# Four inner products of the first matrix product in two levels, with units that accumulate on banks filled by ScalarE and VectorE

## The chip, the cores and the metric

The kernel runs on one core of one Trainium2 chip. The metric is the device time of one execution in microseconds (us). Its engines are TensorE (PE, matrix products; PEld is its loading of weights), VectorE (DVE), ScalarE (ACT), GpSimd (POOL) and SyncE (SP). The last two issue most of the DMAs here.

## What is computed

```python
# q, k, v: (B, H, S, D) = (4, 8, 768, 64), lam: (8,), all fp32
for b in range(S // 64):                           # lightning attention, block by block
    intra = (qb @ kb^T * Dmask) @ vb               # Dmask[i, j] = lam^(i - j) for i >= j
    inter = (qb * lam^(pos + 1)) @ kv_state
    out[block] = intra + inter
    kv_state = lam^64 * kv_state + (kb * lam^(63 - pos))^T @ vb
x = out as (B*S, H*D) = (3072, 512)
h = x @ w_in                                       # w_in  (512, 2048): the first matrix product
g = h - tanh(h)
return g @ w_out                                   # w_out (2048, 512): the second matrix product
```

## The kernel before

**Groups and units.** The kernel takes the sequence in 128-token blocks. Six groups (`NG`) of 512 tokens, one block of each of the four batches, go one after another: `g` is 0 to 5. The hidden width of 2048 is cut into four units (`NU`, `u` is 0 to 3) of 512. Group 0 is the startup, with plain products while the weights arrive. Group 1 uses one-level products throughout. Groups 2 to 5 (`g >= GI`) are the steady state.

**Seven products for eight.** Both matrix products are computed by the scheme with seven block products P1 to P7 in place of eight. The operands of each are sums and differences of quarters: `FACT` names them, S1 to S4 on one side and T1 to T4 on the other. The four result quarters are called 11, 12, 21 and 22. With P1 as a base, C11 = P1 + P2, and P1 + P6 is shared: C12 adds P5 and P3 to it, C22 adds P7 and P5, C21 adds P7 and P4. `hidden(g, c)` is the buffer in SBUF of quarter c of the hidden layer; a one-level product is done there unit by unit, in `up(g, u, n)`, with 8 matmul records of 256 columns a unit.

**Two levels.** A block product can be split by the same scheme once more. It is then seven steps of 8 records of 128 columns, in the order `STEPS` = 1, 2, 6, 5, 7, 3, 4, over all four units at once. For the second matrix product, `down_twice` (L697) does so for P3 to P7 (`TWICE`), and `down` (L684) keeps P1 and P2 at one level. For the first, `inner_steps(g, n, tag)` (L518) does so for P2 and P4 (`INNER`, groups from 2 on). Its result goes into `hidden` quarter 11 or 21 through ScalarE copies and VectorE additions. `inner_weights` (in group 1) makes the factors of the weights, four VectorE operations of 128x128 a unit and product, and stores them in `fine_in`; `inner_tokens` makes those of the tokens, four operations a product.

**The steady state.** At the seam of two groups, P3 of the second product of group g alternates with the inner steps of P2 of group g+1 (`in_turn`); then come the inner steps of P4, with P1, P6 and P5 of unit 0 between them. The unit loop follows, in the order P7, P3 for a unit and P6, P5, P1 for the next. P5 of a unit goes to the PSUM bank `z`, P3 is accumulated upon it, and P1, P6 and P7 are accumulated on `ya` or `yb` by the parity of u. VectorE adds the pieces up in `hidden`, ScalarE takes the tanh (L454) and VectorE subtracts it (L455). After P3 the sums S1 and S2 of the second product are made (L482 and the line behind it). Then follows the second product, P1 (`every(down(g, 1))` as the last act of the unit loop, in bank `ya`), P2 in bank `w`, P4, P5, P6 and P7. Between them run the pieces of attention for group g+1, by halves of two batches each: `att_transpose` (for g >= 2 a VectorE transpose of blocks that 16 DMAs on SyncE's queue load per tile, L143), `att_scores` (L333), `att_out`, `att_state` and the token sums `att_sums`. Transposes and scores of batches 0 and 1 stand in the unit loop (`run(p0[u - 2:u - 1])`).

**PSUM.** There are eight banks of 128x512: `ya`, `yb`, `z` and `w` with one buffer each, and four under the tag `att`, which attention and the inner steps take in turn.

**Weights.** The factors for the second product lie in DRAM (`factors` for one level, `fine` and `fine_in` for two levels). `piece` (L620, L623) issues their loads of 256 KB on GpSimd's queue, in the order of `stream`, into a ring `wb` of seven tiles (`RING`), as the tile used seven pieces earlier comes free. The two-level factors themselves are made in groups 1 and 2 by `load_quarters` and `factors_twice`: VectorE subtracts quarters of `factors`, and GpSimd stores each result in `fine` (L604, L614). In group 2 these quarters go through the same ring, and the stream has all twelve of them ahead of P1's four pieces.

**What orders the work.** The program's text gives the order by generators that are advanced step by step. A scheduler may move an instruction of an engine past another when their operands allow, save where `keep_in_program_order` ties it. So P7 and P3 of a unit, for instance, stand around the matmuls of other units in the built order.

Of the kernel before, what the change touches and what calls it, by code (L numbers as in the profile page):

```python
# [24 lines left out]
def kernel(  # L25
# [32 lines left out]
    nc = tc.nc  # L58
# [127 lines left out]
    TWICE = (3, 5, 6, 4, 7)  # L186
    fine = dram.tile([len(TWICE), len(SUB), 128, NU, 128], F32, name="fine")

    fine_in = dram.tile([2, 3, 128, NU, 128], F32, name="fine_in")
    w_in_u = moe_w_in.rearrange("k (a n) -> k a n", a=2)  # L190
    blocks = [("in", u, i) for u in range(NU) for i in range(KI)] + [("out", kt, a) for kt in range(KH)
                                                                    for a in range(2)]
# [244 lines left out]
    def up(g, u, n):  # L437
        a, bname = FACT[n]
        wt = {"A11": w1[u][:, 0:2, 0], "A12": w1[u][:, 2:4, 0], "S3": w1[u][:, 0:2, 1], "A22": w1[u][:, 2:4, 1],
              "S1": ws[u][:, 0], "S2": ws[u][:, 1], "S4": ws[u][:, 2]}[a]  # L440
        x = xt[g][bname] if bname != "B11" else xt[g, 0][:, 0:2]
        key = ("up", g, u)
        t, first = product_bank(key, n)
        for m in range(2):
            for kt in range(2):
                nc.tensor.matmul(out=t[:, m, :], lhsT=wt[:, kt, ts(m, 128)], rhs=x[:, kt, :],  # L446
                                 start=first and m == 0 and kt == 0, stop=kt == 1, skip_group_check=True)

        def dst(c):
            return hidden(g, c)[:, u]  # L450

        def finish(c, src):
            th = work.tile([128, 2, HB], F32, name="th", tag="th")
            nc.scalar.activation(th, src, AF.Tanh)  # L454
            nc.vector.tensor_tensor(dst(c), src, th, op=AL.subtract)  # L455

        y, z, w = (banks[key, x].rearrange("q (m c) -> q m c", m=2) if (key, x) in banks else None for x in "yzw")
        if g >= GI and n == 1:
            nc.vector.tensor_tensor(dst(11), dst(11), y, op=AL.add)  # L459
            finish(11, dst(11))  # L460
        elif g >= GI and n == 5:
            nc.scalar.activation(dst(22), z, AF.Copy)  # L462
        elif g >= GI and n == 7:
            nc.vector.tensor_tensor(dst(22), dst(22), y, op=AL.add)
            nc.vector.tensor_tensor(dst(21), dst(21), y, op=AL.add)
            finish(22, dst(22))
            finish(21, dst(21))
        elif n == 1:
            nc.scalar.activation(dst(11), y, AF.Copy)
        elif n == 2:  # L470
            nc.vector.tensor_tensor(dst(11), dst(11), w, op=AL.add)
            finish(11, dst(11))
        elif n == 6:
            nc.scalar.activation(dst(12), y, AF.Copy)
        elif n == 7:
            nc.scalar.activation(dst(22), y, AF.Copy)
            nc.vector.tensor_tensor(dst(22), dst(22), z, op=AL.add)
            finish(22, dst(22))
        elif n == 4:
            finish(21, y)  # L480
        elif n == 3:
            nc.vector.tensor_tensor(dst(12), dst(12), z, op=AL.add)  # L482
            finish(12, dst(12))

            nc.vector.tensor_tensor(dst("S1"), dst(12), dst(22), op=AL.add)
            nc.vector.tensor_tensor(dst(12), dst(11), dst(12), op=AL.subtract)

    INNER = (2, 4)  # L490
    toks = {}

    def a_quarter(n, u, i, k):
        return w1[u][:, 2 + k, INNER.index(n), ts(i, 128)]

    def inner_weights(u):
        for n in INNER:
# [8 lines left out]
    def inner_tokens(g):  # L506
        for n in INNER:
            x = xt[g][FACT[n][1]]
# [9 lines left out]
    def inner_steps(g, n, tag):  # L518

        y, w, z, r5 = bank("y3", tag, 1), bank("w3", "att", 4), bank("z3", "att", 4), otile("r5")  # L520
        out4 = hidden(g, 11 if n == 2 else 21)
        c11, c12, c21, c22 = (out4[:, :, i, ts(j, 128)] for i in range(2) for j in range(2))
        for x in STEPS:
            b = toks[g, n][x]
            wb = piece(g, ("in", n), x) if x in (3, 5, 6) else None
            dst = w if x == 2 else z if x in (3, 5) else y
            for u in range(NU):
                a = wb.rearrange("p m c -> p (m c)")[:, ts(u, 128)] if wb is not None else a_quarter(
                    n, u, *{1: (0, 0), 2: (0, 1), 7: (1, 0), 4: (1, 1)}[x])
                nc.tensor.matmul(out=dst[:, ts(u, 128)], lhsT=a, rhs=b, start=x in (1, 2, 5) and u == 0, stop=True,  # L530
                                 skip_group_check=True)
# [20 lines left out]
    def in_turn(g):  # L552

        if twice(g, 3):
            return [a for x in STEPS for a in (("down", x), ("in", x))]
        return [("down", 0), ("in", 1), ("in", 2), ("down", 1), ("in", 6), ("in", 5), ("down", 2), ("in", 7), ("in", 3),
                ("down", 3), ("in", 4)]

    def pieces_of(g):
        if g >= GI:  # L560
            yield from ((g, ("in", 4), x) for x in (6, 5, 3))
        if g == 2:
            yield from ((g, ("quarter", t), x) for t in (2, 3, 4) for x in range(4))
        for n in (1, 2, 4, 5, 6, 7):
            yield from ((g, n, x) for x in (SUB if twice(g, n) else range(NU)))
        if g == NG - 1:
            yield from ((g, 3, x) for x in range(NU))
# [1 line left out]
        for kind, x in in_turn(g):  # L569
            if kind == "down":  # L570
                yield g, 3, x
            elif x in (3, 5, 6):
                yield g + 1, ("in", 2), x

    stream = [x for g in range(1, NG) for x in pieces_of(g)]
    sent = {"n": 0}
# [66 lines left out]

    def down(g, n):

        if n in (1, 2):
            t, first = product_bank(("down", g), n)
        else:
            t, first = bank("plain", "w" if n == 7 else "z", 1).rearrange("q (m c) -> q m c", m=2), True
# [240 lines left out]
    late["pool"] = ctx.enter_context(tc.tile_pool(name="late", bufs=1))  # L890


    turns = {1: (0, ((0, 7), (1, 14))), 2: (7 * NU, ((2, 1), (3, 5), (4, 9)))}
    made, making = [], {}
    load_quarters(0)
    load_quarters(1)
    up(1, 0, 1)
    for g in range(1, NG):
        last = g == NG - 1
        p0, p1 = attention(g + 1) if not last else ([], [])  # L900
        for u in range(NU):
            for n in (2, 6, 5, 7, 1, 4, 3) if g < GI else (1, 7, 3) if u == 0 else (6, 5, 1, 7, 3) if u + 1 < NU else (
                    6, 5, 7, 1, 3):
                if n != 1:
                    up(g, u, n)
                elif u + 1 < NU:
                    up(g, u + 1, 1)
                else:
                    every(down(g, 1))
                if g == 1 and u < 2 and n == 5:  # L910
                    sums_in(u + 2)
                if g in turns:
                    made.append(n)
                    step = len(made) - turns[g][0]
                    for t, first in turns[g][1]:
                        if step == first:
                            if t > 1:
                                load_quarters(t)
                            making[t] = factors_twice(t)
                        if first <= step < first + 4:  # L920
                            next(making[t])
            if g == GI - 1:
                inner_weights(u)
            if not last and u > 1:
                run(p0[u - 2:u - 1])
        if twice(g, 4):
            sums_twice(g, 4)
        every(down(g, 2))
# [23 lines left out]
        every(p2)  # L952
        every(p3)
        p4 = inner_steps(g + 1, 4, "yb")
        for n in (None, None, 1, None, None, 6, None, None, 5, None):
# [35 lines left out]
```

## Time and profile before

| | |
|---|---|
| time, median of 3 runs | 672.54 us (670.41 to 673.64) |
| span of the profiled execution | 668.3 us |
| that execution's span and the median run | 4.2 us apart |
| PE busy | 655.9 us (98%), 4920 records |
| DVE busy | 466.4 us (70%), 839 instructions |
| ACT busy | 212.4 us (32%), 402 instructions |
| POOL busy | 210.3 us (31%), 365 instructions |
| mean granted TensorE clock | 1.000 |
| bytes moved | 128.82 MB, 193 GB/s over the span |

Two records of PE stand for one fp32 matmul of the program; "busy" counts the time in which an instruction of that engine was in execution. The span runs from the first to the last instruction, and the time of a run includes what lies around the span. Group 0 takes the first 108 us or so, and a steady group about 119 us.

### The profile page before, as it was taken

The numbers are of one execution on the slowest core, as the hardware profiler recorded it, in microseconds if no ns is written. First come the engines' busy times: TensorE is split into PE (matmuls) and PEld (weight loads), VectorE is DVE, ScalarE is ACT, GpSimd is POOL, SyncE is SP. The second block draws the span as 40 slices with busy tenths as digits, with TensorE's granted clock in tenths as the row PEclk, the third lists the DMA queues.
The fourth block names the chain that finished last, engine by engine and source line by source line (L and its number), as shares of the span: only waits on it lengthen the run. The fifth ranks groups of instructions, "written<-read, shape, count | busy, mean of one in ns | idle before, by whom it ended". The sixth has DMA issues, their size and how long they took to land.

```text
span 668.3 us, 13066 instructions
## 1 busy us (share of the span) xinstructions
PE 655.9 (98%) x4920; PEld 594.3 (89%) x4920; DVE 466.4 (70%) x839; ACT 212.4 (32%) x402; POOL 210.3 (31%) x365
## 2 busy tenths in 40 slices
PE   8899899999999999999999999999999999999998
PEld 7688788888888989888999988999988899988897
DVE  4477886746988762599885379987368877357753
ACT  4796835503321111341112343112233112234110
POOL 0001444734522433244435101344300245400351
PEclk9999999999999999999999999999999999999999
DMA  9989887968755977568899543698830576610494
GB/s 211 221 218 259 251 320 227 331 172 239 222 136 144 234 184 209 137 210 260 231 269 279 143 75 81 163 275 252 221 67 18 157 237 220 220 35 0 124 298 162
DMA packets 163038, 128.82 MB, mean 193 GB/s; under 512 B 134176, under 2 KB 135328, under 8 KB 162976
## 3 DMA queue, kind: packets, MB, share of 16 engines
q0 software_dynamic: 29296, 96.49, 44.5%
q1 hardware_dynamic: 133536, 31.50, 24.2%
q8 instruction: 39, 0.64, 0.4%
q14 instruction: 23, 0.19, 0.1%
q10 hardware_dynamic: 144, 0.00, 0.0%
HBM read 103.55 MB, written 24.38 MB: 191 GB/s over the span
## 4 chain that ended last, share of the span: by engine, by line
PE 75%; issue 11%; DMA 5%; POOL 4%; ACT 2%; SPq 2%; DVE 1%; POOLq 0%; DVEq 0%; ACTq 0%
PE y L446 13%; PE z L446 8%; PE y L708 8%; PE acc L792 7%; PE zw L708 6%; PE h L763 5%; PE w L655 4%; PE y L655 4%; PE y L530 4%; PE plain L655 3%; PE sp L340 3%; POOL wb L620 3%; PE op L394 2%; DMA raw<-in_moe_w_in_dram 2%; PE z L530 2%
## 5 line engine op out<-in xcount | busy, mean ns | idle before, releaser
L620 POOL DMA_DIRECT2D wb<-fine x147 | 79.1, 539 | 113.8 <-PE y L708 49.6
L623 POOL DMA_DIRECT2D wb<-factors x56 | 30.3, 541 | 156.0 <-PE y L655 99.7
L454 ACT ACTIVATE th<-g 128x512 f32<-128x512 f32 x76 | 47.6, 630 | 99.1 <-DVE g L459 33.2
L446 PE MATMUL y<-xt,w 128*128 128x256 f32 x320 | 74.0, 380 | 0.0
L446 PEld LDWEIGHTS y<-xt,w 128*128 128x128 f32 x320 | 59.9, 190 | 8.5 <-ACT g L534 0.9
L711 ACT ACTIVATE q<-y 128x128 f32<-128x128 f32 x84 | 23.3, 277 | 129.9 <-PE y L708 126.2
L455 DVE TENSOR_TENSOR g<-g,th 128x512 f32<-128x512 f32 x76 | 51.8, 687 | 16.8 <-ACT th L454 16.7
L763 PE MATMUL h<-xt,w 128*128 128x256 f32 x256 | 57.9, 382 | 3.0 <-DVE w L284 3.0
L763 PEld LDWEIGHTS h<-xt,w 128*128 128x128 f32 x256 | 47.7, 190 | 10.7 <-DVE w L284 3.4
L708 PE MATMUL y<-wb,g 128*128 128x128 f32 x384 | 51.1, 278 | 0.0
L708 PEld LDWEIGHTS y<-wb,g 128*128 128x128 f32 x384 | 46.4, 192 | 1.2 <-issue 0.3
L446 PE MATMUL z<-tt,ws 128*128 128x256 f32 x160 | 38.0, 380 | 0.0
L446 PE MATMUL z<-xt,ws 128*128 128x256 f32 x160 | 37.9, 380 | 0.0
L446 PE MATMUL y<-tt,ws 128*128 128x256 f32 x160 | 37.8, 379 | 0.0
L655 PE MATMUL y<-wb,g 128*128 128x256 f32 x160 | 35.6, 379 | 0.5 <-PE y L446 0.5
L655 PE MATMUL w<-wb,g 128*128 128x256 f32 x160 | 35.8, 382 | 0.0
L205 POOL DMA_DIRECT2D raw<-in_moe_w_out_dram x16 | 8.7, 547 | 85.0 <-ACT r L281 60.6
L344 DVE TENSOR_TENSOR ss<-sp,mask 128x512 f32<-128x512 f32 x48 | 30.9, 681 | 6.3 <-PE sp L340 6.3
L655 PEld LDWEIGHTS y<-wb,g 128*128 128x128 f32 x160 | 30.3, 190 | 5.0 <-PE y L446 0.9
L446 PEld LDWEIGHTS z<-xt,ws 128*128 128x128 f32 x160 | 30.3, 190 | 4.3 <-ACT g L462 0.2
L655 PEld LDWEIGHTS w<-wb,g 128*128 128x128 f32 x160 | 30.1, 190 | 4.4
L708 PE MATMUL zw<-wb,g 128*128 128x128 f32 x256 | 33.8, 275 | 0.0
(198 smaller groups left out, 1348.7 us busy)
## 6 DMA issues: line engine op xcount, KB each, us to landing
wb<-fine POOLq DMA_DIRECT2D x147, 256.0 KB, 4.0
wb<-factors POOLq DMA_DIRECT2D x68, 256.0 KB, 4.1
raw<-in_moe_w_out_dram POOLq DMA_DIRECT2D x16, 512.0 KB, 5.8
v_nat<-in_v_dram SPq DMA_DIRECT2D x24, 256.0 KB, 5.1
fine<-wt POOLq DMA_DIRECT2D x24, 256.0 KB, 4.8
wb<-fine_in POOLq DMA_DIRECT2D x24, 256.0 KB, 4.1
k_nat<-in_k_dram SPq DMA_DIRECT2D x20, 256.0 KB, 4.9
raw<-in_moe_w_in_dram SPq DMA_DIRECT2D x8, 512.0 KB, 5.7
```

The lines of the kernel that those rows point to most:

```text
L344: tied(g == 0, nc.vector.tensor_tensor(ss[:, j], sp[j], mask[:, j], op=AL.mult))
L446: nc.tensor.matmul(out=t[:, m, :], lhsT=wt[:, kt, ts(m, 128)], rhs=x[:, kt, :], start=first and m == 0 and kt == 0, stop=kt == 1, skip_gro ...
L454: nc.scalar.activation(th, src, AF.Tanh)
L455: nc.vector.tensor_tensor(dst(c), src, th, op=AL.subtract)
L530: nc.tensor.matmul(out=dst[:, ts(u, 128)], lhsT=a, rhs=b, start=x in (1, 2, 5) and u == 0, stop=True, skip_group_check=True)
L620: nc.gpsimd.dma_start(out=t.rearrange("p m c -> p (m c)"), in_=fine[TWICE.index(n_), SUB.index(x_)].rearrange("p u c -> p (u c)"))
L623: nc.gpsimd.dma_start(out=t, in_=factors[XAT[FACT[n_][1]]][:, 2 * x_:2 * x_ + 2, :])
L655: nc.tensor.matmul(out=t[:, m, :], lhsT=a[:, u, kt, ts(m, 128)], rhs=wb[:, kt, :], start=first and u == 0 and m == 0 and kt == 0, stop=u = ...
L708: nc.tensor.matmul(out=dst, lhsT=a[:, u, :], rhs=wb[:, ts(u, 128)], start=x in (1, 2) and u == 0, stop=u == NU - 1, skip_group_check=True)
L711: nc.scalar.activation(keep, dst, AF.Copy)
L763: tied(u == 0, nc.tensor.matmul(out=hm[c][:, m, :], lhsT=w1[u][:, i, a, ts(m, 128)], rhs=xt[0, t][:, i, :], start=m == 0 and i == 0, stop= ...
L792: nc.tensor.matmul(out=acc[n][:, r, :], lhsT=a[:, ts(r, 128)], rhs=b, start=kt == 0 and r == 0, stop=kt == KH - 1, skip_group_check=True)
```

## The change

P1 and P5 of the first product join P2 and P4 in two levels for the groups 2 to 5: `INNER` becomes (1, 5, 2, 4). In the unit loop of these groups only P6, P3 and P7 are left, in a new function `seeded`.

- For P6 of a unit, ScalarE copies quarter 12 of `hidden`, where the inner steps of P1 landed, into bank `ya` or `yb`, and the matmuls accumulate on that. VectorE then writes the bank's content plus quarter 22 (where P5 landed) into a second bank, `z` for even and `w` for odd units, and P3's matmuls accumulate there. P7 accumulates on the first bank. The second bank's content goes through tanh, and a VectorE subtraction that reads the bank writes C12.
- C11 is P1's landing (12) plus P2's landing (11). It is finished by VectorE and ScalarE (`n == 11`) beside the inner steps of P4.
- P1 of the second product takes an `att` bank, and its four units are spread over the unit loop. The pieces of `stream` in group 2 follow that order: P1's piece, four quarters, P1's next piece.
- The inner steps of P1 alternate with P3 of the second product, those of P5 and P2 alternate with each other, and P6 of units 0 and 1 and P3 of unit 0 stand among the steps of P4.
- The transposes and scores of batches 0 and 1 move from the unit loop of group g to the seam ahead of it, as `early_pieces` for group g+2.

In the built program, PE has 128 matmuls of 256 columns fewer and 224 of 128 columns more (2492 to 2588 in all), VectorE has 88 additions, subtractions and the like more (733 to 821), ScalarE 16 instructions more (401 to 417), GpSimd 32 DMAs more (359 to 391), and SyncE as many as before.

```diff
-    fine_in = dram.tile([2, 3, 128, NU, 128], F32, name="fine_in")
+    INNER = (1, 5, 2, 4)
+    fine_in = dram.tile([len(INNER), 3, 128, NU, 128], F32, name="fine_in")
...
-    INNER = (2, 4)
+    LAND = {1: 12, 5: 22, 2: 11, 4: 21}
+    BANKS = {1: ("yb", "w", "att"), 5: ("ya", "att", "z"), 2: ("yb", "w", "att"), 4: ("att", "att", "att")}
+    def seeded(g, u, n):
...
+        if n == 11:
+            nc.vector.tensor_tensor(dst(11), dst(11), dst(12), op=AL.add)
+            finish(11, dst(11))
+            return
+        if n == 6:
+            banks[g, u, "y"] = bank("y", "yb" if u % 2 else "ya", 1).rearrange("q (m c) -> q m c", m=2)
+            nc.scalar.activation(banks[g, u, "y"], dst(12), AF.Copy)
+        y = banks[g, u, "y"]
+        t = banks[g, u, "z"] if n == 3 else y
...
+        for m in range(2):
+            for kt in range(2):
+                nc.tensor.matmul(out=t[:, m, :], lhsT=wt[:, kt, ts(m, 128)], rhs=x[:, kt, :], start=False,
+                                 stop=kt == 1, skip_group_check=True)
+        if n == 6:
+            z = banks[g, u, "z"] = bank("zs", "w" if u % 2 else "z", 1).rearrange("q (m c) -> q m c", m=2)
+            nc.vector.tensor_tensor(z, y, dst(22), op=AL.add)
+        elif n == 3:
+            finish(12, t)
+        else:
+            nc.vector.tensor_tensor(dst(22), dst(22), y, op=AL.add)
+            nc.vector.tensor_tensor(dst(21), dst(21), y, op=AL.add)
+            finish(22, dst(22))
+            finish(21, dst(21))
+    def seeded_sums(g, u):
+        g11, g12, g22, s1 = (hidden(g, c)[:, u] for c in (11, 12, 22, "S1"))
+        nc.vector.tensor_tensor(s1, g12, g22, op=AL.add)
+        nc.vector.tensor_tensor(g12, g11, g12, op=AL.subtract)
...
     def pieces_of(g):
         if g >= GI:
             yield from ((g, ("in", 4), x) for x in (6, 5, 3))
-        if g == 2:
-            yield from ((g, ("quarter", t), x) for t in (2, 3, 4) for x in range(4))
-        for n in (1, 2, 4, 5, 6, 7):
+        for u in range(NU):
+            yield g, 1, u
+            if g == 2 and u + 1 < NU:
+                yield from ((g, ("quarter", u + 2), x) for x in range(4))
+        for n in (2, 4, 5, 6, 7):
             yield from ((g, n, x) for x in (SUB if twice(g, n) else range(NU)))
...
-        if n in (1, 2):
+        if n == 1 and g >= GI:
+            t, first = bank("plain", "att", 4).rearrange("q (m c) -> q m c", m=2), True
...
+            if u == 0:
+                first = down(g, 1)
+            for n in (1, 7) if u == 0 else (6, 3, 1, 7) if u + 1 < NU else (7, 3, 1):
+                if n == 1:
+                    next(first)
                 else:
-                    every(down(g, 1))
...
+                    seeded(g, u + (n == 6), n)
+                if n == (7 if u + 1 < NU else 3):
+                    seeded_sums(g, u)
...
-        inner_tokens(g + 1)
+        ahead = attention(g + 2) if g + 2 < NG else ([], [])
+        early_pieces = [(fn, g + 2, (b,)) for fn in (att_transpose, att_scores) for b in (0, 1)] if g + 2 < NG else []
+        inner_tokens(g + 1, (1, 5))
         p3 = down_twice(g, 3, "z") if twice(g, 3) else down(g, 3)
-        p2 = inner_steps(g + 1, 2, "yb")
-        for kind, _ in in_turn(g):
-            next(p3 if kind == "down" else p2)
...
+        parts = {"down": p3}
+        for i, (kind, x) in enumerate(in_turn(g)):
+            if kind == 2 and x == 1:
+                inner_tokens(g + 1, (2,))
+            if kind not in parts:
+                parts[kind] = inner_steps(g + 1, kind)
+            next(parts[kind])
+            if kind == 1 and x in (6, 7, 4):
+                run(early_pieces[:1])
+                early_pieces = early_pieces[1:]
+            if kind == 2 and x == 6:
+                run(early_pieces)
...
+        inner_tokens(g + 1, (4,))
+        p4 = inner_steps(g + 1, 4)
+        for n in (None, None, 6, None, None, 16, None, None, 3, None):
             if n is None:
                 next(p4)
             else:
-                up(g + 1, 0, n)
+                seeded(g + 1, n // 10, n % 10)
+                seeded(g + 1, (6, 16, 3).index(n), 11)
+        seeded(g + 1, 3, 11)
         every(p4)
```

More of the change, by code (lines that the diff above doesn't have):

```diff
@@ L457, in up @@
         y, z, w = (banks[key, x].rearrange("q (m c) -> q m c", m=2) if (key, x) in banks else None for x in "yzw")
[L458 to L468, printed above, removed]
+        if n == 1:
             nc.scalar.activation(dst(11), y, AF.Copy)
@@ L486, in up, with dst, finish @@
             nc.vector.tensor_tensor(dst(12), dst(11), dst(12), op=AL.subtract)
-    INNER = (2, 4)
     toks = {}
+    LAND = {1: 12, 5: 22, 2: 11, 4: 21}
+    BANKS = {1: ("yb", "w", "att"), 5: ("ya", "att", "z"), 2: ("yb", "w", "att"), 4: ("att", "att", "att")}
+    def seeded(g, u, n):
+        def dst(c):
+            return hidden(g, c)[:, u]
+        def finish(c, src):
+            th = work.tile([128, 2, HB], F32, name="th", tag="th")
+            nc.scalar.activation(th, src, AF.Tanh)
+            nc.vector.tensor_tensor(dst(c), src, th, op=AL.subtract)
+        if n == 11:
[7 more added lines that the diff above has]
+        t = banks[g, u, "z"] if n == 3 else y
+        a, bname = FACT[n]
+        wt = {"S3": w1[u][:, 0:2, 1], "S2": ws[u][:, 1], "S4": ws[u][:, 2]}[a]
+        x = xt[g][bname]
+        for m in range(2):
[16 more added lines that the diff above has]
+        nc.vector.tensor_tensor(g12, g11, g12, op=AL.subtract)
     def a_quarter(n, u, i, k):
-        return w1[u][:, 2 + k, INNER.index(n), ts(i, 128)]
+        wt = {1: w1[u][:, 0:2, 0], 2: w1[u][:, 2:4, 0], 4: w1[u][:, 2:4, 1], 5: ws[u][:, 0]}[n]
+        return wt[:, k, ts(i, 128)]
     def inner_weights(u):
@@ L504, in inner_weights, with inner_tokens @@
             nc.gpsimd.dma_start(out=fine_in[INNER.index(n)].rearrange("x p u c -> p u x c")[:, u], in_=t[:, 0:3])
-    def inner_tokens(g):
-        for n in INNER:
-            x = xt[g][FACT[n][1]]
+    def inner_tokens(g, ns):
+        for n in ns:
+            x = xt[g][FACT[n][1]] if n != 1 else xt[g, 0][:, 0:2]
             b11, b12, b21, b22 = (x[:, k, ts(j, 128)] for k in range(2) for j in range(2))
@@ L516, with inner_steps @@
     STEPS = (1, 2, 6, 5, 7, 3, 4)
-    def inner_steps(g, n, tag):
-        y, w, z, r5 = bank("y3", tag, 1), bank("w3", "att", 4), bank("z3", "att", 4), otile("r5")
-        out4 = hidden(g, 11 if n == 2 else 21)
+    def inner_steps(g, n):
+        y, w, z = (bank(x, tag, 4 if tag == "att" else 1) for x, tag in zip(("y3", "w3", "z3"), BANKS[n]))
+        r5 = otile("r5")
+        out4 = hidden(g, LAND[n])
         c11, c12, c21, c22 = (out4[:, :, i, ts(j, 128)] for i in range(2) for j in range(2))
@@ L554, in in_turn @@
         if twice(g, 3):
-            return [a for x in STEPS for a in (("down", x), ("in", x))]
-        return [("down", 0), ("in", 1), ("in", 2), ("down", 1), ("in", 6), ("in", 5), ("down", 2), ("in", 7), ("in", 3),
-                ("down", 3), ("in", 4)]
+            turn = [a for x in STEPS for a in (("down", x), (1, x))]
+        else:
+            turn = [("down", 0), (1, 1), (1, 2), ("down", 1), (1, 6), (1, 5), ("down", 2), (1, 7), (1, 3), ("down", 3),
+                    (1, 4)]
+        return turn + [(n, x) for x in STEPS for n in (5, 2)]
     def pieces_of(g):
@@ L572, in pieces_of @@
             elif x in (3, 5, 6):
-                yield g + 1, ("in", 2), x
+                yield g + 1, ("in", kind), x
     stream = [x for g in range(1, NG) for x in pieces_of(g)]
@@ L644, in down @@
     def down(g, n):
-        if n in (1, 2):
+        if n == 1 and g >= GI:
+            t, first = bank("plain", "att", 4).rearrange("q (m c) -> q m c", m=2), True
+        elif n in (1, 2):
             t, first = product_bank(("down", g), n)
@@ L890, with make_factors @@
     late["pool"] = ctx.enter_context(tc.tile_pool(name="late", bufs=1))
-    turns = {1: (0, ((0, 7), (1, 14))), 2: (7 * NU, ((2, 1), (3, 5), (4, 9)))}
-    made, making = [], {}
+    TURNS = {1: ((0, 7), (1, 14)), 2: ((2, 1), (3, 5), (4, 9))}
+    making = {}
+    def make_factors(g, step):
+        for t, first in TURNS.get(g, ()):
+            if step == first:
+                if t > 1:
+                    load_quarters(t)
+                making[t] = factors_twice(t)
+            if first <= step < first + 4:
+                next(making[t])
     load_quarters(0)
@@ L897 @@
     up(1, 0, 1)
+    ahead = attention(2)
     for g in range(1, NG):
         last = g == NG - 1
-        p0, p1 = attention(g + 1) if not last else ([], [])
+        (p0, p1), step = ahead, 0
         for u in range(NU):
[L902 to L907, printed above, removed]
-                else:
-                    every(down(g, 1))
[L910 to L925, printed above, removed]
+            if g < GI:
+                for n in (2, 6, 5, 7, 1, 4, 3):
+                    if n != 1:
+                        up(g, u, n)
+                    elif u + 1 < NU:
+                        up(g, u + 1, 1)
+                    else:
+                        every(down(g, 1))
+                    if u < 2 and n == 5:
+                        sums_in(u + 2)
+                    step += 1
+                    make_factors(g, step)
+                inner_weights(u)
+                if u > 1:
+                    run(p0[u - 2:u - 1])
+                continue
+            if u == 0:
+                first = down(g, 1)
+            for n in (1, 7) if u == 0 else (6, 3, 1, 7) if u + 1 < NU else (7, 3, 1):
+                if n == 1:
+                    next(first)
+                else:
+                    seeded(g, u + (n == 6), n)
+                if n == (7 if u + 1 < NU else 3):
+                    seeded_sums(g, u)
+                step += 1
+                make_factors(g, step)
         if twice(g, 4):
@@ L946 @@
             continue
-        inner_tokens(g + 1)
+        ahead = attention(g + 2) if g + 2 < NG else ([], [])
+        early_pieces = [(fn, g + 2, (b,)) for fn in (att_transpose, att_scores) for b in (0, 1)] if g + 2 < NG else []
+        inner_tokens(g + 1, (1, 5))
         p3 = down_twice(g, 3, "z") if twice(g, 3) else down(g, 3)
-        p2 = inner_steps(g + 1, 2, "yb")
-        for kind, _ in in_turn(g):
-            next(p3 if kind == "down" else p2)
[L952 to L955, printed above, removed]
+        parts = {"down": p3}
[10 more added lines that the diff above has]
+                run(early_pieces)
+        for p in parts.values():
+            every(p)
+        inner_tokens(g + 1, (4,))
+        p4 = inner_steps(g + 1, 4)
+        for n in (None, None, 6, None, None, 16, None, None, 3, None):
             if n is None:
```

## The prediction

> **What bounds the kernel now.** The page comes first: its busy times and its issue table.
>
> ```profile
> PE 655.9 (98%) x4920; PEld 594.3 (89%) x4920; DVE 466.4 (70%) x839; ACT 212.4 (32%) x402; POOL 210.3 (31%) x365
> ...
> wb<-factors POOLq DMA_DIRECT2D x68, 256.0 KB, 4.1
> ```
>
> TensorE has 12 us without a matmul in 668, most of them before group 1. Its work therefore sets the time, and whatever makes it wait adds in full. A weight piece takes 4.1 us from issue to landing. Next is the chain of waits, at the seam of groups 3 and 4 (start, length, instructions).
>
> ```profile
> 475.25 0.95 PE y L530 x8
> 476.21 1.73 PE y L446 x8
> 477.94 0.89 PE y L530 x8
> ...
> 513.63 6.91 PE y L655 x32
> 520.54 1.73 PE z L446 x8
> 522.26 1.99 PE sp L340 x32
> ```
>
> These are the prices of TensorE: a unit of a one-level product is 8 records of 256 columns and 1.73 us, a step of a two-level product 8 records of 128 columns and 0.89 us, a whole one-level product 6.91 us. Starts touch, so nothing waits. (The page's "mean ns of one", 380 and 278, overlaps with the neighbours and is not a price.) The timeline of all engines gives the others.
>
> ```profile
> 379.91 3.71 PE L446 MATMUL y<-xt,w 128*128 128x256 f32 x16
> ...
> 383.73 0.69 DVE L464 TENSOR_TENSOR g<-g,y 128x512 f32<-128x512 f32 x1 [0.25 <-PE y L446]
> 384.33 0.68 DVE L455 TENSOR_TENSOR g<-g,th 128x512 f32<-128x512 f32 x1
> 384.94 0.68 DVE L465 TENSOR_TENSOR g<-g,y 128x512 f32<-128x512 f32 x1
> ...
> 386.91 0.63 ACT L454 ACTIVATE th<-g 128x512 f32<-128x512 f32 x1 [0.57 <-DVE g L482]
> 387.44 0.58 ACT L474 ACTIVATE g<-y 128x512 f32<-128x512 f32 x1
> ```
>
> VectorE starts one 128x512 operation every 0.60 us, ScalarE every 0.53 to 0.55. A reader starts 0.11 us after the matmuls' end at 383.62; that end is 0.17 later than the slot of the next matmul, so a VectorE reader starts 0.28 us after TensorE has gone on. The timelines of TensorE and GpSimd in group 2 show the one thin place.
>
> ```profile
> 298.95 0.67 PE L655 MATMUL y<-wb,g 128*128 128x256 f32 x2 [0.53 <-PE y L446]
> ```
>
> ```profile
> 291.54 0.76 POOL L614 DMA_DIRECT2D wb<-factors  x1 [2.08 <-DMA fine<-wb]
> 292.29 0.55 POOL L604 DMA_DIRECT2D fine<-wt  x1
> 292.82 0.55 POOL L623 DMA_DIRECT2D wb<-factors  x1
> 293.35 0.54 POOL L604 DMA_DIRECT2D fine<-wb  x1
> 298.69 0.54 POOL L623 DMA_DIRECT2D wb<-factors  x1 [4.80 <-DMA fine<-wb]
> ```
>
> While the second-level weight factors are made, GpSimd's queue stands twice for a store to end (4.8 us the second time), and P1's first piece, issued at 292.82, lands 5.6 us later: TensorE loses 0.53 us.
>
> **The change, part by part.** t is us from the start of P4's first inner step (261.7 in group 2 now).
>
> *Fewer matmuls.* P1 and P5 of groups 2 to 5 go from 4 units x 1.73 = 6.91 us to 7 steps x 0.89 = 6.26 us: 0.65 us, eight times, -5.2 us on the bounding engine. No other matmul is added or removed. [...]
>
> *Added work off TensorE.* VectorE gets 24 inner additions (0.60) and 64 quarter sums of 128x128 (0.20 from start to start in its timeline), 27 us in all; ScalarE 16 copies, 9 us; GpSimd 24 piece loads and 8 stores. The inner steps of P5 and P2 alternate, so a bank is read over 3 x 0.89 = 2.7 us against a copy of 0.6: hidden. 32 of the quarter sums, 8 per unit, fall to group 1, where P5's factors, used at 224.9, are ready at 215: some 2 us more in a unit's queue are covered. The six more pieces per group stand in 12.5 us that need six, where the 12.5 us before need ten: zero, and 24 x 0.85 us if DMA (1.03 busy at 461 to 474) had no room.
>
> *Banks filled by ScalarE and VectorE.* P6 of unit 2 needs, after P7 of unit 0 (ends t = 14.9): two additions (15.2 to 16.5), tanh of C21 (to 17.1) and the copy into the bank (17.05 to 17.6). TensorE has P3 of unit 1 and three quarters of a P1 unit meanwhile, and comes at 17.9. Unit 3: ready 24.6, wanted 24.85. Hidden with 0.25 us to spare; P3's fill comes 0.8 us early. Cost 0, at most 0.4 twice a group if the handover is slower.
>
> *The wait for bank w.* P3 of units 1 and 3 now accumulates in w, and the first-product P2 of `down` needs that bank. Unit 3's C12 is finished by a VectorE subtraction that reads w itself, and in the built order it is the twelfth operation after P7 of unit 2. VectorE: 0.28 + 12 x 0.60 + 0.4 (two tanh not ready) + 0.1 = 8.0 us. TensorE over the same stretch, groups 3 and 4: three units 5.19, `op` from the state 1.03, a quarter of `op` from the scores 0.48 = 6.7. It waits 1.3 us, twice. Group 5 has two P4 steps there instead of attention: 5.19 + 1.79 = 7.0, a wait of 1.0. In group 2 the next term makes TensorE later than VectorE. Sum +3.6 us. Bounds: 1.8 (VectorE needs only 0.55 us) to 6.
>
> *Group 2's pieces.* P1's pieces now stand between the quarters in GpSimd's queue, and VectorE has 12 factor operations among the 30 of the units. P1's third piece waits for a slot that the in-place quarter subtraction frees: VectorE reaches it at t = 20.8 and ends at 21.5, issue 21.7, landing about 5 later (between the 4.1 of the table and the 5.6 above): 26.6. TensorE is there at 24.4: 2.2 us. The fourth piece stands behind a wait for a store (22.2 to 27.2), behind the quarter whose slot the third piece holds (30.3) and behind the next in-place subtraction (30.8): issue 31.0, landing 36.0, wanted 34.4: 1.6 us. Sum +3.8; the 0.53 above goes: -0.5. Bounds 0.5 (landing in 3 us) to 8. [...]
>
> *A stage sooner.* The transposes and scores of batches 0 and 1 leave the unit loop and go between inner steps, so VectorE's queue there is 10 operations shorter in groups 2 to 4 (taken into the counts above). Their matmuls cost the same. C11's finish goes beside P4's inner steps, where VectorE has room. The transposes need block loads that SP issues one tile after another.
>
> ```profile
> 430.06 11.14 SPq L143 DMA_DIRECT2D q_blk<-in_q_dram  x16
> 441.24 9.34 SPq L143 DMA_DIRECT2D k_blk<-in_k_dram  x16
> 450.63 9.18 SPq L143 DMA_DIRECT2D q_blk<-in_q_dram  x16
> 459.90 8.53 SPq L143 DMA_DIRECT2D k_blk<-in_k_dram  x16
> ```
>
> Batch 1's keys land at 468.4 + 3.5 = 471.9, 10.2 us after P3 starts (461.7); VectorE gets to them after 9.8. TensorE next needs VectorE at 18.9, and the queue between takes 4.3: 4.4 us to spare. Cost 0.
>
> *Sum:* -5.2 - 0.5 + 3.6 + 3.8 = +1.7 us on the profiled span of 668.3, 670.0; with the 4.2 us by which the median run (672.54) is above that span, **674.2 us**. That is no change: 0.5%, 3.4 us, is about what a measurement here can tell.
>
> **The rivals.** *The new waits don't show.* VectorE orders its tail so that bank w is free in time and the pieces land: -5.7, 666.8 us. For it: the chain of before hides almost all such waits. Against it: the twelve operations are counted, and 0.60 us each is a row. 0.27, since VectorE needs to gain only 1.3 us on a count of twelve.
>
> *The quarter chain lands on TensorE (slower).* Place: GpSimd's queue in group 2. Each of the two waits for a store to end (2.1 and 4.8 us idle now) becomes TensorE's, since P1's pieces stand behind them: 10 us for 3.8, 680.4. It decides if the in-place subtraction is reached after t = 23. For it: VectorE has 42 operations x 0.6 = 25 us in that stretch of 24. 0.16.
>
> *Transposes block VectorE (slower).* If the four block tiles take 11.95 us each, as the slowest tile of the trace, batch 1's keys come 9.4 us later in group 3 and 12 in group 2: 5 and 6.5 us past what is to spare, 685.7. It decides once the keys land over 14.6 us after P3 starts. Against it: 8.9 and 9.6 us a tile in the same stretch now. 0.08.
>
> *Half-width matmuls cost more than half.* With the 278 and 380 ns of the page as prices, 56 x 0.278 against 32 x 0.380 is 3.4 us lost per product, 700. The starts refute it: 0.01.
>
> **How the numbers follow.** The forecast, a saving that the new waits take back, has the remaining 0.48, with 669.5 to 678 as its own range. Its low end gives 0.02 to faster, and its high end, above 675.9, gives 0.08 to slower: faster 0.27 + 0.02 = 0.29, slower 0.16 + 0.08 + 0.01 + 0.08 = 0.33, same 0.38. The range 666 to 681 takes in the first two rivals' times; it leaves out some of each beyond those ends (0.1 together) and the last two: about 0.2.
>
> **What would show it.** Right: gaps in front of the first matmul of P2 (L697, bank w) of 1.3 us in groups 3 and 4 and 1.0 in group 5, ended by VectorE's subtraction (L493); gaps of some 2 us before P1's third and fourth unit in group 2, ended by a DMA; P1 and P5 in steps of 0.89. Wrong: no such gaps and a span near 663, or TensorE idle for a transpose (L320) at a seam.

## The result and the profile after

| | before | after |
|---|---|---|
| time, median (13 runs each) | 670.78 us (669.74 to 673.64) | 678.12 us (672.86 to 689.29) |
| ratio, 95% interval | | 1.008 [1.0054, 1.0107] |
| profiled execution: span | 668.3 us | 674.6 us |
| its PE busy | 655.9 us | 655.0 us |

The change makes the kernel 0.8% slower. Two of the thirteen runs after (687.22 and 689.29 us) had a lower TensorE clock (0.989 and 0.990, for 0.995 to 1.000 in the others), and the ratio leaves them out. In these runs the time is the span and 1.8 to 3.0 us more, mostly 1.8 to 2.0; the profiled execution after took 676.44.

The page of the kernel after, first part, clock row and DMA issues:

```profile
PE 655.0 (97%) x5112; PEld 598.0 (89%) x5112; DVE 493.0 (73%) x927; ACT 218.4 (32%) x418; POOL 229.2 (34%) x397
...
PEclk9999999999899999999999999999999999999999
...
wb<-factors POOLq DMA_DIRECT2D x68, 256.0 KB, 4.3
```

TensorE's busy time fell by 0.9 us only, not by the 5.2 us of the shorter products. The records at half rate (below, the 8 in the clock row) take back 1.8, and since the ends of matmuls are modelled, the first 0.16 us of each pause counts as busy; what is left was not taken apart. VectorE has 26.6 us more, as was counted (27). The span has 19.6 us without a matmul where it had 12.4.

The chain of waits of the kernel after at the seam of groups 3 and 4 (start, length, instructions), and at the end of group 4's unit loop:

```profile
498.80 1.73 PE y L509 x8
500.53 0.89 PE y L566 x8
501.42 0.89 PE z L566 x8
...
530.89 0.67 DVE g L493 x2
531.56 0.45 issue
532.01 0.69 DVE s L734
532.70 0.61 DVE g L493
533.31 0.04 issue
533.35 7.17 PE w L697 x32
```

The steps of the inner products cost 0.89 us and the units 1.73, so the saving of 0.65 us a product is there. But the chain leaves TensorE at the end of the unit loop and comes back only with P2 of the second product: the wait for bank `w`.

The waits of TensorE in the kernel after (engine, line, waited for: us in total, times, longest), startup's left out:

```profile
PE y L750 <- DMA wb<-fine: 2.3, 2, 1.4
PE w L697 <- DVE g L493: 2.3, 4, 0.8
PE plain L697 <- DMA wb<-factors: 1.8, 2, 1.1
PE y L447 <- DVE g L456: 1.7, 1, 1.7
...
PE sp L341 <- DVE ss L345: 0.6, 1, 0.6
```

The same view of the kernel before had, outside the startup, only these over 0.2 us:

```profile
PE y L708 <- DMA wb<-fine: 0.7, 1, 0.7
PE y L655 <- PE y L446: 0.5, 1, 0.5
PE kv L362 <- PE op L394: 0.3, 1, 0.3
```

To say where the 6.3 us of span lie, a landmark helps that is the same work in both: the first matmul of the state part of `att_out` for batches 2 and 3, in group 2. From the timelines of TensorE, first the kernel after, then the kernel before:

```profile
351.64 1.10 PE L389 MATMUL op<-qd,state 64*64 64x128 f32 x32
```

```profile
345.70 1.10 PE L388 MATMUL op<-qd,state 64*64 64x128 f32 x32
```

The landmark is 5.9 us late. From it to the last matmul (671.2 and 664.9) the kernel after needs 319.6 us for the 319.2 of before, although three of the four pairs of shorter products lie there: 3 x 1.3 = 3.9 saved and 4.3 given back. Up to it, one pair saves 1.3; the startup was by chance 1.0 shorter; so groups 1 and 2 together gave back 8.2.

Group 1. The timelines of VectorE and of TensorE in the kernel after:

```profile
168.54 0.68 DVE L468 TENSOR_TENSOR g<-g,z 128x512 f32<-128x512 f32 x1
171.33 0.29 DVE L538 TENSOR_TENSOR ws<-w 128x128 f32<-128x128 f32 x1 [2.10 <-DMA fine_in<-ws]
```

```profile
174.23 1.89 PE L447 MATMUL y<-tt,ws 128*128 128x256 f32 x8
177.82 0.70 PE L447 MATMUL y<-xt,w 128*128 128x256 f32 x2 [1.70 <-DVE g L456]
178.41 3.11 PE L447 MATMUL z<-tt,ws 128*128 128x256 f32 x8
```

In unit 1 VectorE stands 2.10 us for a store to DRAM, because the quarter sums of unit 0 now use four tiles under the tag `sums`, and there are four. It also has eight more quarter sums in that queue. It frees banks `y` and `z` late, TensorE waits (1.86 us by the starts, 1.70 by the model's ends), and then the eight records at 178.41 take 3.11 us where such a group takes 1.89 elsewhere, as at 174.23: from 179.2 to 182.6 each of eight records takes 427 ns in place of 216. That costs another 1.8 us.

Group 2. GpSimd's timeline in the kernel after, and TensorE's:

```profile
295.34 0.56 POOL L644 DMA_DIRECT2D fine<-wt  x1
300.60 0.56 POOL L644 DMA_DIRECT2D fine<-wt  x1 [4.70 <-DVE wt L643]
301.14 0.76 POOL L654 DMA_DIRECT2D wb<-factors  x1
301.89 0.55 POOL L663 DMA_DIRECT2D wb<-factors  x1
```

```profile
305.72 1.13 PE L697 MATMUL plain<-wb,g 128*128 128x256 f32 x4 [1.11 <-DMA wb<-factors]
```

P1's third piece is issued at 301.89 and TensorE goes on at 305.72, 3.8 us later. Ahead of it in the queue stands a store that waited 4.70 us for VectorE's second subtraction. The third subtraction, in place, by which the prediction had the piece's tile come free, ended hardly sooner than the issue. From VectorE's timeline:

```profile
300.82 0.69 DVE L643 TENSOR_TENSOR wb<-wb 128x512 f32<-128x512 f32 x1
```

Both were late because VectorE reached the second subtraction 6.0 us after the first (299.61 and 293.62).

### The profile page after: what moved, and what is told of

It is laid out like the page before. It is cut to its first block, busy times and chain, and to the rows that moved or that the text cites. A ratio compares the mean times of both kernels' runs of the same rounds, so it can differ in the third digit from the quotient of the medians.

```text
span 674.6 us, 13667 instructions
## 1 busy us (share of the span) xinstructions
PE 655.0 (97%) x5112; PEld 598.0 (89%) x5112; DVE 493.0 (73%) x927; ACT 218.4 (32%) x418; POOL 229.2 (34%) x397
## 4 chain that ended last, share of the span: by engine, by line
PE 58%; DMA 12%; SPq 8%; issue 8%; DVE 5%; ACT 4%; POOL 3%; POOLq 0%; ACTq 0%; DVEq 0%
PE y L750 8%; PE y L509 6%; SPq L143 6%; PE zw L750 6%; PE y L566 5%; PE w L697 5%; PE plain L697 5%; DMA q_blk<-in_q_dram 4%; PE z L566 3%; PE h L805 3%; PE zs L509 3%; DMA k_blk<-in_k_dram 2%; PE sp L341 2%; PE op L395 2%; DMA raw<-in_moe_w_in_dram 2%
## 5 line engine op out<-in xcount | busy, mean ns | idle before, releaser
L697 PE MATMUL plain<-wb,g 128*128 128x256 f32 x224 | 53.5, 381 | 1.8 <-DMA wb<-factors 1.8
L750 PE MATMUL y<-wb,g 128*128 128x128 f32 x384 | 51.4, 278 | 0.0
L697 PEld LDWEIGHTS plain<-wb,g 128*128 128x128 f32 x224 | 41.7, 190 | 8.0 <-DMA wb<-factors 2.6
L570 ACT ACTIVATE g<-y 128x512 f32<-128x512 f32 x48 | 28.5, 594 | 60.8 <-PE y L566 60.2
L492 ACT ACTIVATE th<-g 128x512 f32<-128x512 f32 x48 | 29.3, 628 | 57.9 <-DVE g L517 53.9
L750 PEld LDWEIGHTS y<-wb,g 128*128 128x128 f32 x384 | 46.5, 192 | 1.5 <-issue 0.5
L657 POOL DMA_DIRECT2D wb<-fine_in x48 | 26.0, 541 | 39.6 <-PE y L566 14.6
L750 PE MATMUL zw<-wb,g 128*128 128x128 f32 x256 | 33.8, 275 | 0.0
L493 DVE TENSOR_TENSOR g<-g,th 128x512 f32<-128x512 f32 x48 | 31.7, 688 | 2.7 <-ACT th L492 2.7
L834 PE MATMUL acc<-wt,g 128*128 128x256 f32 x144 | 32.7, 380 | 0.0
L750 PEld LDWEIGHTS zw<-wb,g 128*128 128x128 f32 x256 | 31.2, 192 | 0.0
L834 PEld LDWEIGHTS acc<-wt,g 128*128 128x128 f32 x144 | 27.2, 190 | 3.8 <-DVE g L841 0.2
```

Of the source, the lines that this page charges most:

```text
L697: nc.tensor.matmul(out=t[:, m, :], lhsT=a[:, u, kt, ts(m, 128)], rhs=wb[:, kt, :], start=first and u == 0 and m == 0 and kt == 0, stop=u = ...
L750: nc.tensor.matmul(out=dst, lhsT=a[:, u, :], rhs=wb[:, ts(u, 128)], start=x in (1, 2) and u == 0, stop=u == NU - 1, skip_group_check=True)
L834: nc.tensor.matmul(out=acc[n][:, r, :], lhsT=a[:, ts(r, 128)], rhs=b, start=kt == 0 and r == 0, stop=kt == KH - 1, skip_group_check=True)
```

## The experiments

In the expectations, "span" is the profiled execution's. Gaps are taken from the starts of TensorE's records, and the ratio is against the kernel before, with its 95% interval.

### The group-1 wait

**The weight factors alone, on the kernel before.**

```diff
     def inner_weights(u):
-        for n in INNER:
+        for n in (1, 5, 2, 4):
...
-(a21, a11, a21, AL.subtract),
+(a21 if n in INNER else t[:, 3], a11, a21, AL.subtract),
```

> The kernel before the change with nothing of it but the weight factors: in group 1 the quarter sums of P1 and P5 are made and stored in DRAM too, and not used (their in-place sum goes to the tile's free quarter). Theory (group 1's queue): the 32 additional VectorE operations and eight stores make TensorE wait 1.5 to 1.9 us in unit 1 of group 1, for VectorE's read of bank `z`, and nothing else changes: span 1.5 to 2 us longer than before, 670 to 670.5, or some 672 where records at half rate follow the wait. Rival (the new units are needed for it): without the new order of groups 2 to 5 VectorE catches up in time: no gap over 0.5 us in group 1 and the span as before, 668.3.

Span 669.9, ratio 1.0034 [1.0012, 1.0055]. One gap of 1.53 us appeared, in unit 1 of group 1, and no record at half rate followed it. From the timeline of TensorE:

```profile
177.69 0.70 PE L446 MATMUL y<-xt,w 128*128 128x256 f32 x2 [1.37 <-DVE g L455]
178.28 1.99 PE L446 MATMUL z<-tt,ws 128*128 128x256 f32 x8
```

The first theory holds: the new factors cost group 1 some 1.5 us whatever groups 2 to 5 do.

**Five tiles.** On the kernel after:

```diff
-... name="ws2", tag="sums", bufs=4)
+... name="ws2", tag="sums", bufs=5)
```

(and in the three other places with that tag)

> The changed kernel with five tiles in place of four under the tag `sums`, from which the inner weight factors, the two-level factors and the token sums are taken in turn. Theory (tiles): in group 1 the added quarter sums take twice as many of these tiles, and VectorE stands 2.1 us for the store of an earlier tile to end; TensorE's 1.86 us gap and its 4 us at about half rate behind it come from that. Then the gap shrinks below 0.5 us, no records run at half rate, and the span falls by some 3.8 us, to about 671. Rival (queue): it is the number of VectorE operations in unit 1 of group 1, which is the same here: the gap stays at 1.5 to 1.9 us and the span at 674 to 675. Rival (moved): the wait for a store goes to the next unit's sums, and half of the gain is lost, 672.5.

Span 672.0, ratio 1.0056 [1.0034, 1.0078]. VectorE's wait for the store went from 2.10 to 1.03 us and the gap from 1.86 to 1.26 only; no half rate followed in this execution. Neither pure theory holds: a shorter wait for the store shortened the gap by 0.6 us, and that the longer queue makes the rest is argued here; the run with unit 3's sums sooner bears on it. In group 2 the gap at P1's third unit was 2.61 us in this execution, for 1.27 in the kernel after.

**P2's and P4's factors later.** With P2 in an `att` bank (below):

```diff
-                inner_weights(u)
+                inner_weights(u, (1, 5))
...
+        if g == GI - 1:
+            inner_weights(0, (2, 4))
         every(down(g, 2))
```

(and units 1 to 3 behind the next products)

> P2 in an `att` bank as in the run before, and the inner weight factors of P2 and P4 made after the unit loop of group 1, so that only those of P1 and P5 are left in it (as many operations and stores per unit as before the change). Theory (group 1's queue): the gap of 1.5 us in group 1 goes; span 1.5 us below that of P2 in an `att` bank alone (668.5), 667. Rival (moved): the eight stores now delay the pieces or VectorE between the second product's steps of group 1, with gaps of over 1 us from 190 to 260 us: span 668.5 or more.

Span 673.9, ratio 1.0056 [1.0037, 1.0074]. The gap in unit 1 went, and one of 3.66 us came at 216.7, in front of the state's matmuls, which waited for VectorE:

```profile
218.40 0.69 DVE L734 TENSOR_TENSOR s<-gS 128x512 f32<-128x512 f32 x1 [1.67 <-DMA fine_in<-ws]
```

In VectorE's timeline the next taker of a `sums` tile stands for the same kind of store. The rival holds: the wait moved and more than doubled.

**Sums of unit 3 sooner.** With P2 in an `att` bank and a ring of eight:

```diff
-                    if u < 2 and n == 5:
-                        sums_in(u + 2)
+                    if u == 0 and n in (5, 4):
+                        sums_in(2 if n == 5 else 3)
```

> P2 in an `att` bank, a ring of eight, and in group 1 the four sums of unit 3's weights (L250, 2.4 us of VectorE) made in unit 0 in place of unit 1. Theory (VectorE's queue in unit 1 of group 1): it has 2.4 us less there, and the gap of 1.44 us goes: span 665.7. Rival (unit 0 has no room, or the store's wait alone is enough): a gap of 1 us or more stays in unit 0 or 1: span 667.

Span 668.8, ratio 1.001 [0.9986, 1.0035]. The gap of 1.44 became 0.95: half a microsecond for 2.4 us of VectorE's work less in that unit. VectorE's wait for the store stayed (2.14 us). The gap neither went, as the theory had it, nor stayed at the rival's 1 us; the queue's length is a part of it. The execution also had a half-rate stretch, in group 2, behind a pause of 2.03 at P1.

### The wait for bank w

**P2 in an `att` bank.**

```diff
-        if n == 1 and g >= GI:
+        if n in (1, 2) and g >= GI:
```

> The changed kernel with P2 of the second product in an `att` bank in groups 2 to 5 in place of bank `w`. Theory (bank w): the waits of 1.01, 1.01 and 0.59 us in front of P2 in groups 3, 4 and 5 are for VectorE to read bank `w`, and they go: span 2.6 us shorter, 672.0. Rival (next in line): P2 now stands ahead of the state's matmuls, and TensorE waits as long for hidden quarter 21 of the last unit or for P4's sums: span 674 to 675, with new gaps inside P2 or in front of P4.

Span 668.5, ratio 1.0015 [0.9998, 1.0033]: 6.1 us below the span after. The three gaps in front of P2 (1.01, 1.01, 0.59) are gone, and no gap over 0.26 us is left in groups 3 to 5. TensorE's timeline in group 3 runs from P1's last unit straight through P2's first (29 records of the two in this window), into the attention matmuls:

```profile
422.80 6.42 PE L697 MATMUL plain<-wb,g 128*128 128x256 f32 x29
...
429.15 1.10 PE L389 MATMUL op<-qd,state 64*64 64x128 f32 x32
```

The theory holds, with 2.6 us. The rest of the 6.1 comes from elsewhere: the half rate did not occur (1.8), the gaps in group 2 fell from 4.5 to 3.7, a wait behind a late key block at the seam of groups 2 and 3 (0.81) and one for a piece in group 3 (1.13, now 0.24) did not come, and the startup was 0.9 longer. How much of that belongs to the edit is open. Over the runs the ratio fell from 1.008 to 1.0015, some 4.4 us, so more than the 2.6 came with it.

### Group 2's pieces

**P1's pieces ahead of one more run of quarters.**

```diff
-            if g == 2 and u + 1 < NU:
-                yield from ((g, ("quarter", u + 2), x) for x in range(4))
+            if g == 2 and 0 < u:
+                yield from ((g, ("quarter", u + 1), x) for x in range(4))
```

> The changed kernel with each of P1's second to fourth pieces in group 2 put one run of four quarters further ahead in GpSimd's queue (P1, P1, quarters, P1, quarters, P1, quarters). Theory (queue order): the third and fourth pieces were late because they stood behind the chain of quarters; the gaps of 1.27 and 0.86 us go and nothing takes their place: span 2.1 us shorter, 672.5. Rival (the chain is the bound): the last quarters are made as much later, and the pieces of P2 and of the two-level products behind them: the 1.54 us gap in group 2 grows to 3 or more and the span stays at 674 to 675.

Span 672.3, ratio 1.0093 [1.0063, 1.0123]. Both gaps at P1 went. But TensorE then came that much sooner to bank `w` in front of P2 and waited 2.43 us there for VectorE, for 0.38 in the kernel after. A half-rate stretch followed, and the 1.54 us gap stayed (1.57). Neither theory holds: something took the place of the gaps, but not the gap that the rival named. It was the next wait in line, for VectorE.

**A ring of eight tiles**, with P2 in an `att` bank:

```diff
-    RING = 7
+    RING = 8
```

> P2 in an `att` bank, and a ring of eight tiles in place of seven for the weight pieces. Theory (ring): P1's third and fourth pieces in group 2 wait for a tile that a quarter's in-place subtraction frees, and one more tile frees it sooner: the gaps of 1.18, 0.74 and 0.87 us in group 2 become less than half as long together; span 667. Rival (store waits): GpSimd stands at the stores of the factors, whatever the ring: the gaps stay within 0.5 us of that and the span at 668.5.

Span 667.1, ratio 0.9991 [0.9968, 1.0013]. In group 2 the theory failed: one gap of 2.04 us stands at P1 and 1.60 at L750, for VectorE, which stood 2.87 us for a store; together with two small ones 4.5 us, no less than with seven. Groups 3 to 5 have no gap over 0.2 us left. By the landmark (TensorE's timeline)

```profile
350.02 1.10 PE L389 MATMUL op<-qd,state 64*64 64x128 f32 x32
```

the rest takes 663.8 - 350.0 = 313.8 us, 5.4 less than before, and up to it the kernel is 4.3 later than before: groups 1 and 2 eat what the steady state gains.

**The subtractions of a set at one step**, on top of that:

```diff
-            if first <= step < first + 4:
+            if g == 2 and step == first:
+                every(making[t])
+            elif g < 2 and first <= step < first + 4:
                 next(making[t])
```

> P2 in an `att` bank, a ring of eight, and in group 2 the four subtractions of each set of two-level factors at one step of the unit loop, in place of one each at four steps. Theory (GpSimd stands for VectorE): P1's third piece was late because a store ahead of it in GpSimd's queue waited 4.7 us for a subtraction that VectorE reached 6 us after the one before; with the four together that wait is below 2 us, the gap of 2.04 us at P1 shrinks below 0.7 us, span 667.1 - 1.4 = 665.7. Rival (tiles): the stores now end too late for the four `sums` tiles, VectorE waits for them, and a gap of over 1 us stands elsewhere in group 2: span 667 or more.

Span 669.1, ratio 1.0004 [0.9982, 1.0026]. GpSimd's timeline:

```profile
299.58 0.76 POOL L654 DMA_DIRECT2D wb<-factors  x1 [1.53 <-issue]
304.10 1.50 POOL L654 DMA_DIRECT2D wb<-factors  x2 [3.75 <-DMA fine<-wb]
```

It now stands 3.75 us for a store to end where it had stood for VectorE, and the gap at P1 is 2.59, with half rate behind it. The theory fails. The wait that the rival named is there: VectorE stands 0.57, 0.80 and 1.09 us in front of three subtractions, each until 0.1 us after the store of an earlier factor has landed. The gap it leads to stands at P1 still, not elsewhere.

**Both orders changed** (this one and unit 3's sums sooner):

> The two before together. If both theories hold, span 664.3, a median some 0.6% below that of the kernel before; each that fails leaves 1.4 us.

Span 668.9, ratio 0.9992 [0.9964, 1.0019]. Group 1's gap was 0.84; group 2 had 2.04 (P6 waiting for ScalarE to fill its bank, after VectorE had stood 1.94 us ahead of a subtraction, until the store of an earlier factor had landed) with half rate behind it, and 1.14. Neither theory brought its 1.4.

**Later factors and a ring of eight:**

> All three: P2 in an `att` bank, the inner weight factors of P2 and P4 later, and a ring of eight. If the waits are independent, span 668.5 - 1.5 - 1.5 = 665.5, 2.8 below that of the kernel before (668.3), and no gap over 1 us behind the startup. If one wait hides the other, 667 to 668.

Span 671.8, ratio 1.0051 [1.0029, 1.0074]: the gap moved to 214.7 (3.51 us), as with seven tiles. The waits are not independent.

### The move of transposes and scores

```diff
+            if not last and u > 1:
+                run(p0[u - 2:u - 1])
...
-        early_pieces = [...] if g + 2 < NG else []
+        early_pieces = [...][:0]
```

> The changed kernel with the transposes and scores of batches 0 and 1 back in the unit loop, as before the change. Theory (VectorE's room): ten VectorE operations of 0.60 to 0.69 us return to the unit loop, and the wait for bank `w` in front of P2 grows from 1.0 to between 2 and 5 us a group in groups 2, 3 and 4: span 677 to 686. Rival (the move was a loss): only the wait of 0.81 us for a late key block at the seam of groups 2 and 3 goes: span 673.8.

Span 676.8, ratio 1.0129 [1.0106, 1.0152]. Gaps in groups 2 to 4 came in front of the scores (waiting for the transposes), of `op` and of P2: 1.5 us in group 3 and the same in group 4, where the kernel after has 1.0, and 1.12 + 0.70 + 1.89 in group 2 for 0.38, with half rate behind the last. The move earns its place in the span, by 2.2 us, though by less than the lower end expected (the ratios' intervals, from 1.0106 here and to 1.0107 above, just touch), and its own cost, the late key block (0.81 us at the seam of groups 2 and 3), went.

### The ring alone

The kernel before with `RING = 8`:

> The kernel before with a ring of eight tiles, and nothing else. It tells whether what the runs with a ring of eight gain is the change's: the kernel before has gaps of 0.69 and 0.87 us that end with a DMA, so 1.5 us at most is to be had, span 666.8 to 668.3.

Span 668.2 with a half-rate stretch in the startup (some 1.7 us), median 669.56, ratio 0.9961 [0.9938, 0.9983]. In groups 2 to 5 the gap of 0.87 became 0.44, and those of 0.24 and 0.29 went: 1.0 us. This is the lowest ratio of all, though its interval overlaps with those of the best versions of the change: none of them beats it, and those (0.9991 and 0.9992) can't be told from the kernel before.

## Why the prediction was right and wrong

The range of 666 to 681 held the time, and the mechanisms were mostly the right ones. The named case, no change at 674.2, was not what came: 0.8% slower, beyond the 0.5%. That the range held is in part luck. Terms that were put at nothing came to 6.6 us; bank `w`, the pieces and the gap came out 2.5 us below their forecast and the startup 1.0, which hid a part of it. The high end of the range had been set for the quarter chain, not for group 1. By the steps:

| term | forecast | profile after |
|---|---|---|
| fewer matmuls | -5.2 | -5.2 (0.89 a step, 1.73 a unit) |
| gap at 298 goes | -0.5 | -0.7 |
| wait for bank w, groups 3, 4, 5 | 1.3 + 1.3 + 1.0 | 1.01 + 1.01 + 0.59, and 0.38 in group 2 |
| P1's pieces in group 2 | 2.2 + 1.6 | 1.27 + 0.86 |
| weight factors in group 1 | 0 | 1.9, and 1.8 of half rate |
| GpSimd's queue behind P1, group 2 | 0 | 1.8 more than before (1.54, 0.30 and 0.20 for 0.24) |
| seam of groups 2 and 3, pieces in group 3 | 0 | 0.81, and 1.13 for 0.87 |
| startup | 0 | -1.0, by chance |
| smaller delays | 0 | the rest, some 1.5, not taken apart |
| sum | +1.7 | +6.3 |

*Fewer matmuls* was right: the starts after are the same 0.89 us a step and 1.73 a unit as before.

*The wait for bank w* was right in place, releaser (L493) and, within 0.4 us each, in size. The count was sound: in group 4 the subtraction that reads `w` is the twelfth operation. In groups 3 and 4 the wait was forecast 0.3 too long.

*Group 2's pieces* were right in place and too large: 2.1 for 3.8. The third piece landed 3.8 us after its issue, not 5; the 4.1 of the DMA table was the better value. The reason given, a tile that the in-place subtraction frees, is not the whole: that subtraction ended 0.4 us before the issue, and a store in front of the piece had waited for the subtraction before it. The run that took the store's wait away did not shorten the gap, so which of the two binds is not shown.

*Added work off TensorE* is the step that failed. "Some 2 us more in a unit's queue are covered", it said, and counted VectorE's operations against the due time of P5's factors. It did not follow the queue into unit 1, where `sums_in` and the two-level factors already stand, nor count the tiles: twice as many stores from four tiles make VectorE wait for DRAM (2.10 us). The factors alone cost 1.5 us (ratio 1.0034); a fifth tile took 0.6 us off the gap, and 2.4 us less work 0.5.

*The quarter chain* was a rival at 680.4. Its mechanism is what the 1.8 us behind P1 look like, and the runs that tried to shorten the chain show that VectorE, the stores and the ring take turns as its bound (VectorE 2.87 us for a store with eight tiles, GpSimd 3.75 for one with the subtractions at one step). Its price was not reached in the profile, and it did not follow from the two waits named, 6.9 us together and not 10.

*Transposes block VectorE* happened once and small, at the seam of groups 2 and 3. From the timelines of SyncE and VectorE there:

```profile
328.45 16.99 SPq L143 DMA_DIRECT2D q_blk<-in_q_dram  x16
345.49 7.68 SPq L143 DMA_DIRECT2D k_blk<-in_k_dram  x16
353.43 10.39 SPq L143 DMA_DIRECT2D q_blk<-in_q_dram  x16
363.92 11.32 SPq L143 DMA_DIRECT2D k_blk<-in_k_dram  x16
```

```profile
378.12 0.71 DVE L320 STREAM_TRANSPOSE kt<-k_blk 128x512 f32<-128x512 f32 x1 [5.74 <-DMA k_blk<-in_k_dram]
```

The four tiles took 46.8 us, nearly the rival's four times 11.95, and VectorE stood 5.74 us for the keys. TensorE lost only 0.81. So the condition came and the price did not. (The 6.5 us that the rival had for group 2 do not follow from its figures either: 12 less the 4.4 to spare is 7.6.)

*The 4.2 us* around the span was mostly a run longer than the profiled one, not overhead, which is 1.8 to 2.0 us in most later runs; 2 us of the forecast's level came from that, and the ratio is the number to read.

## What to carry to other kernels

When TensorE is busy 98% of the time, count for each added step on another engine also the buffers it takes and the stores that must end before they are free: a tile ring is a queue, and in the run with later factors its wait moved to the next in line on that engine (1.67 us of VectorE, 3.66 of TensorE). A saving in the steady state can be lost in the groups that prepare it; two of six groups gave back 8.2 us here. A wait for one shared PSUM bank was the cheapest to mend: one line, 2.6 us.

## What was not expected of the hardware

The granted clock fell after pauses that look harmless. In the traces here, a stretch of 3.41 us at half rate (clock 0.50 in the kernel after), in which six to eight records take 427 ns for 216 and some 1.7 us are lost, came behind pauses of 1.86, 1.89, 2.03, 2.04, 2.06, 2.43, 2.59 and 3.10 us, and behind 3.51 and 3.66, where small matmuls fill most of the stretch. None came behind others of 1.84, 1.98, 2.04 (twice), 2.34, 2.61, 2.67 and 2.80, and behind group 0 none came behind a pause under 1.8.

Where a pause lies makes a difference in the traces. In the kernel after, the granted clock is 1.00 from 5.06 to 179.14 us, 0.50 to 182.55 and 1.00 again to 674.07: stretches of 174.08, 3.41 and 491.52 us, the outer ones 51 and 144 times as long as the middle one. Two windows of its length each (start and end, length, TensorE's busy time and records, granted clock, DMA share, GB/s), first in the kernel after, at the pause of 1.86 us, then in the run with five tiles, at the pause of 2.61:

```profile
175.73:179.14 3.41, 1.71 (x7) 1.00 0.73 182
179.14:182.55 3.41, 3.41 (x9) 0.50 0.84 240
```

```profile
300.95:304.36 3.41, 2.08 (x10) 1.00 1.03 322
304.36:307.77 3.41, 2.29 (x11) 1.00 0.71 266
```

The first pause lies within one window, in which TensorE is busy for 1.71 us, half of the time, and the next window has half the clock. The second pause is longer, but the edge at 304.36 divides it, with 2.08 and 2.29 us of work in the two windows, and the clock stays at 1.00. In windows counted on like this through the traces of the kernels after and before, one alone between the startup and 660 us has under 2.2 us of work, that at 175.73, and half the clock follows that one alone. In the startup, windows with 1.96 us (after) and 1.87 us (before) kept the clock; how little work it takes is not shown.

So here a wait of some 2 us cost nearly 4: the pause of 1.86 and the 1.8 behind it. The kernel after scatters more than the one before, 672.9 to 680.4 us over its eleven compared runs, for 669.7 to 673.6 over the thirteen before. Their mean clock alone does not explain that (677.67 us at 0.999, 674.93 at 0.997), and the reason stays open.
